# Block-sparse attention with a gated Fourier filter on one core: a reordered opening, work shifted from VectorE to GpSimd and ScalarE, and new places for the first 54 slots

## The chip, the core and the metric

The kernel runs on one core of a Trainium2 chip. A core has a matrix engine (TensorE, PE in the profile, with its weight loads as PEld), three engines for elementwise work (VectorE or DVE, ScalarE or ACT, GpSimd or POOL) and a queue engine (SyncE or SP) that issues most of the DMA transfers. Each engine takes its instructions strictly in the order of its own list and waits for others by semaphores. The metric is the device time of one execution in microseconds.

## The reference, cut to what matters

There are 4 batches of 8 heads with 768 positions and 64 values per head. Each query position takes its own block of 64 keys and the three blocks whose mean key scores best for it, under the causal mask. The output of the attention is then projected three times; the second projection goes through a circular convolution along the sequence, given by a filter in the frequency domain, and the three are multiplied and projected once more.

```python
k_rep = k.reshape(B, H, n_blocks, block, D).mean(axis=3)
gate_scores = np.einsum('bhsd,bhnd->bhsn', q, k_rep)
...
top_idx = np.argsort(gate_scores, axis=-1)[..., -top_k:]
...
scores = scale * np.matmul(q, k.transpose(0, 1, 3, 2))
mask = mask & (pos[:, None] >= pos[None, :])
scores = np.where(mask, scores, -1000000000.0)
...
attn = attn / (np.sum(attn, axis=-1, keepdims=True) + 1e-09)
return np.matmul(attn, v).astype(np.float32)
...
x2_conv = np.fft.irfft(X2 * H, n=S, axis=1)
y = x1 * x2_conv * x3
return (y @ w_out).astype(np.float32)
```

## The kernel before

**Tiles.** Two heads form a pair `p`; there are 16 pairs, four to a batch. Keys, queries and values of a pair are loaded as 128 positions by 6 chunks by 2 heads by 64 (`k_nat`, `q_nat`, `v_nat`, one DMA for each head). Scores are made with the keys' positions on the partitions, so that the exponentials (`ex`) can be used as weights of the product with the values.

**Slots.** The work of one head is cut into three groups of score tiles, of 896 columns each. A group is a slot `n`, and there are 96. In a slot, `scores(n + 1)` is issued on PE, then `exponentials(n)` on ACT with a triangle cut on POOL (line 619), then `products(n - 1)` on PE (line 641). At the end of a head DVE takes a reciprocal and scales the output into `xnat` (lines 649 and 650).

**Order.** The order is written out by hand in the dictionary `ORDER`. A number there is seven times the slot plus one of seven places within it, so a step at 109 is issued in slot 15. A key such as `kc0.3` is a step of pair 3; `kc0:3` is the rule for a pair whose number leaves 3 when divided by four. `open` is the list of what comes before slot 0. `first`, `mid` and `last` place the filter part of batches 0, 1 and 2 among the slots of the next batch; the last batch follows in `tail`. `zeros` gives, for a slot, how many matmuls on zeros of 256 columns are issued ahead of its products (line 635); a `w18` in `open` stands for 18 such matmuls of 128 columns (line 188).

**Preparing a pair.**
- `turn_k` transposes three chunks on PE (line 420); for pairs in `summed` PE also multiplies by `sel`, which gives the block sums (line 422). `cast_k` casts on ACT to `KH` (line 439), `sum_k` reduces or copies on DVE to `krs` (lines 446 and 444). `send_k` moves the halves of `KH` to `KA` and `KB`, by the two engines named in `kcopy` (line 453) or by two DMAs.
- `turn_q`, `copy_q` (ACT, `TQL`, line 501) and `rest_q` (DVE, line 506) do the like for queries; `part_q` copies the second head to `QB`, by the engine in `qcopy` (line 528) or a DMA. From pair 5 on a transposing DMA does the turn, after `cast_q` and `split_q` (lines 513 and 518).
- `prep_kr` makes `bd` and `kr` in three small steps (lines 489 to 493), on DVE for pair 0 and on POOL for the others. `prep_gate` multiplies on PE: 15 matmuls at line 541. `prep_mask` takes the best eight (line 550), compares (`lt`, line 553) and clears the own block (`MN`, line 556), `turn_mask` transposes (line 566). For pairs 0 and 1 the mask goes straight to its rows 64 to 75 of `TQL` and `QB` (lines 569, 575 and 581); for later ones ACT copies it to `M16` (line 577) and two DMAs send it on (`send_mask`).
- `mask_rows` writes the fixed rows of `KA` and `KB` on POOL, the other buffers get them by DMA (`buffer_rows`).

**The Fourier matrices** are built in the opening from sines: products on PE (`sp`, line 223), a rounding on ACT (`sr`, `dft_ka`, line 230), a multiple on POOL (`sm`, `dft_kw`, line 236), the rest on PE (`se`), the sine on ACT (`st`). `twists` takes the sine of three small columns (line 210).

**The filter's spectrum** is prepared during batch 0. `filter_fold` reverses a block of 128 rows on PE (`rev`) and makes sum and difference (`fil`, lines 363 and 364), `spectrum` multiplies and copies (lines 379 and 387), `spectrum_turned` turns (lines 400 to 406). `fold` makes sum and difference of the attention's output for the filter (`xf`, lines 678 and 679). The list `swap` names steps that go to another engine than the usual one.

**Who waits for whom in PSUM.** Transposes, gates, masks and spectra share three banks (`one`), score tiles have two places of two banks, and the output `o` has one bank, so the products of a head wait until the head before has been scaled.

Of the kernel before, what the change touches and what calls it, by code (L numbers as in the profile page):

```python
# [9 lines left out]
FP32 = mybir.dt.float32  # L10
FP16 = mybir.dt.float16
BF16 = mybir.dt.bfloat16
AF = mybir.ActivationFunctionType
ALU = mybir.AluOpType
# [64 lines left out]
    "xact": [], "xpe": [0, 1, 2, 3, 7, 11, 15], "mpool": [], "fpool": [],  # L79
# [30 lines left out]
    "zeros": {23: 9, 17: 2, 10: 5, 19: 8, 2: 3, 18: 3, 6: 3, 26: 2, 7: 4, 15: 1, 8: 5, 37: 1,  # L110
        14: 3, 25: 4, 12: 3, 30: 1, 34: 1, 20: 2, 24: 2, 3: 2, 11: 2},
}


# [1 line left out]
def kernel(  # L116
# [10 lines left out]
    nc = tc.nc  # L127

    B, H, S, D = q.shape
    P = 128  # L130
    SC = S // P
    NB = S // 64
    Dm = H * D
# [23 lines left out]
    hy = ctx.enter_context(tc.tile_pool(name="hy", bufs=1))  # L157
# [127 lines left out]
    id16 = const.tile([P, P], fp, name="id16")  # L285
# [86 lines left out]

    spec = {}

    def spectrum(j, which):
        sl = slice(P * j, P * (j + 1))
        hps = one("hps")
        for i in range(HC):
            nc.tensor.matmul(hps, lhsT=(FC, FS)[which][:, i, sl], rhs=fil[:, which, i, :],
                             start=(i == 0), stop=(i == HC - 1))  # L380
        if which:
            hsb = hy2.tile([P, Dm], FP32, name="hsb", tag="h1")
        else:
            hsb = hy.tile([P, 2, F], FP32, name="hsa", tag="yy",
                          bufs=DC - 1).rearrange("p a f -> p (a f)")[:, 0:Dm]
        spec[j, which] = hsb
        (nc.scalar.copy if (which == 1) != (f"ch{which}{j}" in ORDER["swap"]) else nc.vector.tensor_copy)(
            hsb, hps)

    def spectrum_turned(j, what, part):  # L390
        c, s_ = spec[j, 0], spec[j, 1]
        dst, first, s0, second, s1, op = {
            "A": (Asb[:, j, :], c, tw[:, 0, j:j + 1], s_, tw[:, 1, j:j + 1], ALU.add),
            "B": (Bsb[:, j, :], s_, tw0[:, 0:1] if j == 0 else tw[:, 0, j:j + 1], c,
                  tw[:, 1, j:j + 1], ALU.subtract),
            "2": (A2, c, tw0[:, 0:1], s_, tw0[:, 1:2], ALU.add)}[what]
        if part == 0:
            t = hy.tile([P, Dm], FP32, name="turn", tag="t1", bufs=3)
            if f"ct{what}{j}" in ORDER["swap"]:
                nc.scalar.activation(t, second, AF.Copy, bias=0.0, scale=s1)  # L400
            else:
                nc.gpsimd.tensor_scalar(t, in0=second, scalar1=s1, scalar2=0.0, op0=ALU.mult,
                                        op1=ALU.add)
            spec[j, what] = t
        else:
            nc.vector.scalar_tensor_tensor(out=dst, in0=first, scalar=s0, in1=spec.pop((j, what)),
                                           op0=ALU.mult, op1=op)
# [174 lines left out]
                                scalar2=None, op0=ALU.mult)  # L582

    def send_mask(p):
        nc.sync.dma_start(TQ[p % 3][64:64 + NB, :], M16[p % 2][64:64 + NB, :])
        nc.sync.dma_start(QB[p % 2][64:64 + NB, :], M16[p % 2][96:96 + NB, :])

# [407 lines left out]
```

## Time and profile before

| | |
|---|---|
| median of 3 runs | 243.94 us |
| lowest and highest | 243.31 and 243.98 us |
| the profiled execution's own time | 243.25 us |
| its span | 241.5 us |
| granted clock of TensorE | 1.00 |
| first exponential starts at | 13.89 us |
| 27th exponential (slot 26) starts at | 62.98 us |
| moved by DMA | 38.31 MB, 159 GB/s in the mean |

The span runs from the first to the last recorded instruction; 1.75 us of the execution lie around it. A row of the timeline or of the chain gives a start and a duration; a row of the groups gives, after the bar, the busy time in all and the mean in nanoseconds of one, then the idle time of the engine just before, with what ended it. Instructions that follow each other on one engine overlap a little, so their durations add up to slightly more than the time they take. A matmul of 32-bit values shows as two records. The slot of an exponential is counted from the first, slot 0.

### The profile page before, as it was taken

Reading aid. Unit: us, or ns where it says so; the run is one execution under the profiler, and the core shown is the slowest. Engines: PE = TensorE matmul, PEld = TensorE weight load, DVE = VectorE, ACT = ScalarE, POOL = GpSimd, SP = SyncE. Lnnn points to the kernel's source line nnn. Section 1 sums busy time; section 2 is a strip of 40 time slices with the busy share of each in tenths; the row PEclk is TensorE's granted clock in tenths of the full one; section 3 lists DMA queues with packets and bytes.
Section 4 is the critical chain, followed back from the end, with each engine's and each line's share of the span. In section 5 each row is a group of like instructions: output and inputs, shape, how many; then the busy total and the mean of one; then the engine's idle time right before and its main releaser. Section 6 shows DMA issues by size and latency. Waiting matters only on the chain.

```text
span 241.5 us, 6285 instructions
## 1 busy us (share of the span) xinstructions
PE 228.6 (95%) x2277; PEld 149.5 (62%) x2277; DVE 192.8 (80%) x569; ACT 168.2 (70%) x261; POOL 142.6 (59%) x257
## 2 busy tenths in 40 slices
PE   5789999899899999999999999999999999999993
PEld 4578776577666766666566666666655665544551
DVE  3787797999978999887589978986699767578981
ACT  4879878878878867877985777878854866322341
POOL 8725646588873779853445788736365695006560
PEclk9999999999999999999999999999999999999999
DMA  7999979599999999979989999999961012500015
GB/s 156 218 252 237 176 185 198 113 196 176 185 181 170 189 210 168 173 161 261 246 187 203 144 188 188 154 221 273 175 152 36 10 34 79 186 0 0 3 41 220
DMA packets 108679, 38.31 MB, mean 159 GB/s; under 512 B 100596, under 2 KB 104936, under 8 KB 108648
## 3 DMA queue, kind: packets, MB, share of 16 engines
q1 hardware_dynamic: 106248, 35.68, 75.1%
q0 software_dynamic: 2256, 2.10, 5.9%
q8 instruction: 18, 0.29, 0.5%
q10 hardware_dynamic: 144, 0.13, 0.2%
q14 instruction: 13, 0.11, 0.2%
HBM read 24.64 MB, written 6.29 MB: 128 GB/s over the span
## 4 chain that ended last, share of the span: by engine, by line
PE 81%; DVE 11%; ACT 3%; issue 1%; POOL 1%; ACTq 0%; POOLq 0%; DVEq 0%
PE sps L607 13%; PE x2p L704 9%; PE op L780 8%; PE o L641 7%; PE x3p L768 7%; PE x1p L765 7%; PE xx L717 5%; PE kt L420 3%; PE ye L745 3%; PE yo L748 3%; PE o L635 2%; PE mt L566 2%; PE g L541 2%; DVE m L550 2%; ACT ex L616 2%; PE sps L765 1%
## 5 line engine op out<-in xcount | busy, mean ns | idle before, releaser
L616 ACT ACTIVATE ex<-sps 128x896 f16<-128x896 f32 x96 | 87.6, 923 | 1.6 <-PE sps L607 1.2
L619 POOL TENSOR_SCALAR_AFFINE_SELECT ex<-ex 128x256 f16<-128x256 f16 x96 | 42.3, 444 | 55.7 <-ACT ex L616 48.0
L641 PEld LDWEIGHTS <-ex 128*128 128x128 f16 x672 | 32.2, 97 | 10.4 <-DVE xnat L650 1.5
L641 PE MATMUL o<-V,ex 128*128 128x65 f16 x672 | 35.9, 193 | 0.5 <-DVE xnat L650 0.2
L737 POOL TENSOR_TENSOR yT<-gg,yy 128x384 f16<-128x384 f32 x23 | 22.9, 1016 | 8.1 <-DVE yy L754 3.5
L728 POOL TENSOR_TENSOR PQ<-ta 128x512 f16<-128x512 f32 x12 | 15.2, 1269 | 19.7 <-DVE ta L727 19.6
L607 PE MATMUL sps<-QB,KB 76*128 76x512 f16 (+1 forms) x144 | 26.2, 289 | 0.7 <-ACT ex L616 0.6
L607 PE MATMUL sps<-TQL,KA 76*128 76x512 f16 (+1 forms) x144 | 26.2, 289 | 0.6 <-DVE TQL L569 0.4
L771 ACT CAST x1sb<-x1p 128x384 f16<-128x384 f32 x27 | 12.9, 479 | 16.4 <-PE x1p L765 16.4
L704 PE MATMUL x2p<-wp,xf 128*128 128x512 f16 x96 | 23.8, 378 | 0.0
L765 PE MATMUL x1p<-xT,wp 128*128 128x384 f16 x108 | 22.0, 325 | 0.0
L768 PE MATMUL x3p<-xT,wp 128*128 128x384 f16 x108 | 22.0, 326 | 0.0
L780 PE MATMUL op<-wo,yT 128*128 128x512 f16 x84 | 20.7, 379 | 0.0
L439 ACT CAST KH<-kt 128x384 f16<-128x384 f32 x30 | 14.4, 481 | 8.7 <-DVE krs L446 4.4
L773 DVE TENSOR_TENSOR gg<-x1sb,x3p 128x384 f32<-128x384 f16 x27 | 14.8, 549 | 5.5 <-PE x3p L768 4.7
L650 DVE TENSOR_TENSOR xnat<-o,rc 128x384 f16<-128x384 f32 x32 | 17.8, 557 | 1.1
L768 PEld LDWEIGHTS <-wp 128*128 128x128 f16 x128 | 12.5, 98 | 8.6 <-issue 0.2
L607 PEld LDWEIGHTS <-KA 76*128 76x128 f16 x144 | 12.2, 97 | 8.9 <-issue 1.5
L607 PEld LDWEIGHTS <-KB 76*128 76x128 f16 x144 | 12.4, 98 | 8.3 <-issue 0.7
L420 PE MATMUL kt<-id,k_nat 128*128 128x128 f32 x90 | 16.4, 280 | 0.4 <-DVE TQL L506 0.4
L446 DVE TENSOR_REDUCE krs<-kt 128x6 f32<-128x384 f32 x26 | 14.2, 551 | 2.8 <-PE kt L420 2.3
L550 DVE MAX8 m<-g 128x8 f32<-128x12 f32 x160 | 13.8, 158 | 3.2 <-PE g L541 3.2
(184 smaller groups left out, 490.5 us busy)
## 6 DMA issues: line engine op xcount, KB each, us to landing
q_nat<-in_q_dram SPq DMA_DIRECT2D x32, 192.0 KB
k_nat<-in_k_dram SPq DMA_DIRECT2D x32, 192.0 KB
v_nat<-in_v_dram SPq DMA_DIRECT2D x32, 192.0 KB
out_dram<-osb SPq DMA_DIRECT2D x23, 256.0 KB
wp<-in_moe_w_proj_dram POOLq DMA_DIRECT2D x12, 128.0 KB, 4.2
KA<-KH SPq DMA_DIRECT2D x9, 96.0 KB
KB<-KH SPq DMA_DIRECT2D x9, 96.0 KB
fa<-in_moe_filter_fft_dram SPq DMA_DIRECT2D x3, 256.0 KB
```

The lines of the kernel that those rows point to most:

```text
L420: nc.tensor.transpose(y[:, P * c:P * (c + 1)], chunk, id32)
L550: nc.vector.max(m8[:, c, h, :], g[:, c, h, :])
L607: nc.tensor.matmul(t[:, col:col + q1 - q0], lhsT=kk[0:64 + NB, P * kc:P * (kc + 1)], rhs=qq[0:64 + NB, q0:q1], start=True, stop=True, skip ...
L616: nc.scalar.activation(ex, t[:, 0:W], AF.Exp, bias=0.0, scale=EXPS)
L619: nc.gpsimd.affine_select(out=tri, in_=tri, compare_op=ALU.is_ge, fill=0.0, base=0, pattern=[[0, 2], [1, P]], channel_multiplier=-1)
L641: nc.tensor.matmul(o[:, qc, :], lhsT=ex[:, c0:c0 + P], rhs=V16[p % 3][:, kc, h, 0:65], start=first, stop=False, skip_group_check=True)
L650: nc.vector.tensor_tensor(xn[:, :, D * h:D * (h + 1)], o[:, :, 0:D], rc.to_broadcast([P, SC, D]), op=ALU.mult)
L704: nc.tensor.matmul(pa, lhsT=xf[:, eo, dc, P * i:P * (i + 1)], rhs=wp[:, dc, Dm:2 * Dm], start=(dc == 0), stop=(dc == DC - 1))
L737: e.tensor_mul(st["yT"][:, dc, F * hf:F * (hf + 1)], g, yy[:, 1, ::-1] if hf else yy[:, 0, :])
L765: nc.tensor.matmul(x1p, lhsT=wp[:, d2, dsl], rhs=xT[:, d2, hs], start=(d2 == 0), stop=(d2 == DC - 1))
L768: nc.tensor.matmul(x3p, lhsT=wp[:, d2, 2 * Dm + P * dc:2 * Dm + P * (dc + 1)], rhs=xT[:, d2, hs], start=(d2 == 0), stop=(d2 == DC - 1))
L780: nc.tensor.matmul(op, lhsT=st["yT"][:, cc, P * i:P * (i + 1)], rhs=wo[:, cc, :], start=(cc == 0), stop=(cc == DC - 1))
```

## The change

It changes the order and the engines of steps. What is computed stays the same.

- *Opening.* Keys of pair 0 are loaded, transposed, cast and summed ahead of its queries. The cast of a half comes ahead of its sum in the list. The iotas of the Fourier matrices come ahead of `halves` (three memsets of `sel`). One rounding (`sr1`) comes ahead of `twists`. The warm-up matmuls are 18 + 13 + 7 instead of 21 + 2 + 18 + 6. `flip` leaves the opening for slot 3. Both copies of pair 0's keys are POOL's, ahead of `mask_rows`.
- *Keys and queries.* `kcopy` gives both copies of pairs 0 and 3 to POOL, both of pair 2 to DVE, and of pairs 4, 5 and 6 one to ACT and one to DVE. Pair 5 joins `summed`. The copy of pair 6's second queries moves from DVE to ACT; pair 8 gets ACT for it in place of a DMA and pair 7 a DMA in place of ACT.
- *Masks.* Clearing the own block goes to POOL for pairs 1, 6 and 7 (`mpool`). A new table `mcopy` lets engines do `send_mask` in place of DMAs: ACT and DVE for pair 2, POOL for the second half of pairs 6 and 8.
- *Filter and folds.* For the first of three blocks ACT copies `rev` to SBUF and POOL makes sum and difference (`fl0`). One spectrum copy goes from DVE to ACT (`ch00`), one copy of a turned matrix likewise, one turn goes from POOL to ACT. The difference in `fold` is POOL's for pairs 0 and 7 (`fpool`).
- *Fillers.* The matmuls on zeros ahead of products are 45 instead of 66.
- *Places.* Nearly every step of pairs 1 to 8 and of batch 0's filter part gets a new number, mostly off by one to ten. `mid`, `last` and `tail` stay.

Two new forms come with it: `send_mask` with `mcopy`, and a way of turning straight from PSUM (`scaled`, for a `split` entry in `swap`), which no entry asks for.

```diff
-    "kcopy": {0: 'AV', 1: 'VV', 2: 'PV', 3: 'AV', 4: 'AV', 5: 'VP', 6: 'VP'},
-    "qcopy": {0: 'A', 1: 'V', 2: 'P', 3: 'P', 4: 'P', 5: 'A', 6: 'V', 7: 'A'}, "summed": [2, 6],
-    "xact": [], "xpe": [0, 1, 2, 3, 7, 11, 15], "mpool": [], "fpool": [],
-    "open": ["id32", "halves", "lq0", "lk0", "angles", "twists", "sp0", "lk1", "biasl", "lv0",
-        "period", "sp1", "zeros", "sr0", "flip", "sp2", "own", "lq1", "w21", "sr1", "q0", "sm0",
-        "sr2", "qc0", "biasr", "sm2", "q1", "qc1", "sm1", "MN0", "qr0", "qr1", "k0", "k1", "qd",
-        "ks0", "kc0", "se2", "w2", "ks1", "kr", "kc1", "id16", "se1", "kd", "se0", "lv1", "st2",
-        "st0", "st1", "g", "m", "rows", "w18", "mt", "table", "lk2", "ones", "v", "ma", "lq2",
-        "w6", "mb", "sel16", "s", "late"],
+    "kcopy": {1: 'VV', 2: 'VV', 3: 'PP', 4: 'AV', 6: 'AV', 5: 'AV', 0: 'PP'},
+    "qcopy": {0: 'A', 1: 'V', 2: 'P', 3: 'P', 4: 'P', 5: 'A', 6: 'A', 8: 'A'}, "summed": [2, 5, 6],
+    "xact": [], "xpe": [0, 1, 2, 3, 7, 11, 15], "mpool": [1, 6, 7], "fpool": [0, 7],
+    "mcopy": {8: '-P', 6: '-P', 2: 'AV'},
+    "open": ["id32", "angles", "halves", "lk0", "period", "zeros", "sp0", "lq0", "lv0", "biasl",
+        "sp2", "sp1", "sr1", "twists", "sr2", "w18", "own", "biasr", "lq1", "sm2", "lk1", "sr0",
+        "k0", "sm1", "sm0", "kc0", "MN0", "ks0", "k1", "kc1", "ks1", "id16", "q0", "qc0", "q1",
+        "kr", "qr0", "qc1", "qr1", "kd", "qd", "se1", "se2", "se0", "lv1", "g", "st2", "st1",
+        "st0", "lk2", "rows", "ones", "w13", "m", "table", "v", "mt", "sel16", "ma", "w7", "mb",
+        "late", "lq2", "s"],
...
     "swap": ["mP12", "tB2", "tX13", "tP01", "mC1", "tI2", "tO0", "ctB1", "cIS0", "mC3", "mY02",
...
-        "mC4", "cIC1", "ce03", "ce02", "ce11", "ce00"],
...
+        "cIC0", "fl0", "ctB0", "ch00", "ct20", "cIS2", "ce12", "ce10", "ce00"],
...
-    "zeros": {23: 9, 17: 2, 10: 5, 19: 8, 2: 3, 18: 3, 6: 3, 26: 2, 7: 4, 15: 1, 8: 5, 37: 1,
-        14: 3, 25: 4, 12: 3, 30: 1, 34: 1, 20: 2, 24: 2, 3: 2, 11: 2},
+    "zeros": {23: 1, 10: 2, 19: 4, 2: 1, 6: 3, 7: 6, 8: 5, 14: 2, 25: 6, 12: 3, 24: 4, 36: 2,
+        21: 2, 26: 1, 20: 2, 4: 1},
...
     def send_mask(p):
-        nc.sync.dma_start(TQ[p % 3][64:64 + NB, :], M16[p % 2][64:64 + NB, :])
-        nc.sync.dma_start(QB[p % 2][64:64 + NB, :], M16[p % 2][96:96 + NB, :])
+        for i, dst in enumerate((TQ[p % 3], QB[p % 2])):
+            copy = ENGINES.get(ORDER.get("mcopy", {}).get(p, "--")[i], nc.sync.dma_start)
+            copy(dst[64:64 + NB, :], M16[p % 2][64 + 32 * i:64 + 32 * i + NB, :])
```

The function that the first block's fold goes through, as it stands in both:

```python
        if f"fl{i}" in ORDER["swap"]:

            revs = hy.tile([P, Dm], FP32, name="revs", tag="t1", bufs=3)
            nc.scalar.copy(revs, rev)
            rev, add, sub = revs, nc.gpsimd.tensor_add, nc.gpsimd.tensor_sub
        add(fil[:, 0, i, :], fa[:, i, :], rev)
        sub(fil[:, 1, i, :], fa[:, i, :], rev)
```

More of the change, by code (lines that the diff above doesn't have):

```diff
@@ L373, with scaled @@
     spec = {}
+    def scaled(dst, src, by, act):
+        if act:
+            nc.scalar.activation(dst, src, AF.Copy, bias=0.0, scale=by)
+        else:
+            nc.vector.tensor_scalar(dst, in0=src, scalar1=by, scalar2=None, op0=ALU.mult)
     def spectrum(j, which):
@@ L386, in spectrum @@
         spec[j, which] = hsb
+        if j and f"split{j}" in ORDER["swap"]:
+            state["hps", j, which] = hps
+            scaled(hsb, hps, tw[:, 0, j:j + 1], (which == 1) != (f"ch{which}{j}" in ORDER["swap"]))
+            return
         (nc.scalar.copy if (which == 1) != (f"ch{which}{j}" in ORDER["swap"]) else nc.vector.tensor_copy)(
@@ L390, in spectrum_turned @@
     def spectrum_turned(j, what, part):
-        c, s_ = spec[j, 0], spec[j, 1]
+        c, s_ = spec.get((j, 0)), spec.get((j, 1))
         dst, first, s0, second, s1, op = {
@@ L396, in spectrum_turned @@
             "2": (A2, c, tw0[:, 0:1], s_, tw0[:, 1:2], ALU.add)}[what]
+        if j and f"split{j}" in ORDER["swap"]:
+            if part == 0:
+                spec[j, what] = t = hy.tile([P, Dm], FP32, name="turn", tag="t1", bufs=3)
+                scaled(t, state.pop(("hps", j, what == "A")), s1, f"ct{what}{j}" in ORDER["swap"])
+            else:
+                e = nc.vector if f"cg{what}{j}" in ORDER["swap"] else nc.gpsimd
+                e.tensor_tensor(dst, first, spec.pop((j, what)), op=op)
+            return
         if part == 0:
```

84 rows, old and new, of the table ORDER are left out of this document.

## The prediction

> **What bounds the kernel now.** I read the page's busy shares first, then the busy time in six stages cut at points where the chain of waits changes character, then that chain, and last the timeline of the opening.
>
> ```profile
> PE 228.6 (95%) x2277; PEld 149.5 (62%) x2277; DVE 192.8 (80%) x569; ACT 168.2 (70%) x261; POOL 142.6 (59%) x257
> ```
>
> ```profile
> 0.00:13.89 13.89, 9.09 (x92) 7.22 (x93) 7.68 (x48) 8.64 (x16) 9.47 (x33) 1.00 1.13 191
> 13.89:29.10 15.21, 14.09 (x193) 11.76 (x192) 12.68 (x58) 13.46 (x22) 8.60 (x21) 1.00 1.12 237
> 29.10:41.97 12.87, 12.65 (x145) 9.02 (x143) 10.12 (x34) 10.23 (x16) 6.62 (x15) 1.00 0.85 180
> 41.97:50.00 8.03, 6.81 (x82) 4.53 (x80) 7.86 (x26) 6.49 (x9) 4.40 (x10) 1.00 0.67 129
> 50.00:62.98 12.98, 12.86 (x163) 10.30 (x164) 12.21 (x35) 10.52 (x15) 11.72 (x21) 1.00 1.01 188
> 62.98:122.00 59.02, 58.20 (x608) 37.66 (x606) 48.74 (x145) 47.32 (x72) 37.57 (x66) 1.00 1.10 192
> ```
>
> The columns are the stage, its length, then PE, PEld, DVE, ACT, POOL, the granted clock and DMA. After 63 us PE is full (58.20 of 59.02), so whatever is won or lost before that shifts the rest unchanged. Up to 13.89 us no engine is full: that stage is a chain. From 13.89 to 62.98 PE idles 1.12 + 0.22 + 1.22 + 0.12 = 2.7 us in all, and in 41.97 to 50.00 VectorE is the full one (7.86 of 8.03). But "PE busy" here includes matmuls on zeros, and they stand on the chain itself:
>
> ```profile
> 3.83 2.35 PE warm L188 x21
> 7.37 0.94 DVE TQL L506 x2
> 8.31 0.94 DVE krs L446 x2
> 41.97 0.69 DVE fil L363
> 52.11 0.88 PE o L635 x8
> 54.12 0.32 DVE KA L453
> 57.54 0.12 PE kt L422 x2
> 58.84 0.98 PE o L635 x9
> ```
>
> A filler of line 635 costs PE 0.88 / 8 = 0.11 us, a warm-up matmul of line 188 2.35 / 21 = 0.112, and a matmul of line 422 that sums a chunk of keys 0.12 for its two records.
>
> **The opening, up to the first exponential.** These rows set its pace.
>
> ```profile
> 0.82 1.28 ACT L210 ACT_TABLE_LOAD   x1 [0.82 <-PEq L981]
> 1.33 0.10 POOL L256 MEMSET sel<- 128x2 f32 x1
> 1.79 0.44 POOL L199 IOTA vals<- 1x384 f16 x1
> 2.69 1.14 PE L223 MATMUL sps<-vals 1*128 1x384 f16 x3 [2.69 <-POOL vals L201]
> 2.85 0.21 ACT L210 ACTIVATE tw<-twf 128x6 f32<-128x6 f32 x1 [0.75 <-POOL twf L208]
> 3.54 1.25 ACT L230 ACTIVATE dft_ka<-sps 128x384 f32<-128x384 f32 x3 [0.49 <-PE sps L223]
> 5.97 1.16 PE L420 MATMUL qt<-id,q_nat 128*128 128x128 f32 x6
> 6.84 0.87 ACT L501 ACTIVATE TQL<-qt 128x384 f16<-128x384 f32 x2 [2.05 <-PE qt L420]
> 8.80 0.94 ACT L439 CAST KH<-kt 128x384 f16<-128x384 f32 x2 [0.22 <-DVE krs L446]
> 9.27 0.32 DVE L489 TENSOR_TENSOR bd<-krs,sel 128x24 f32<-128x24 f32 x1
> 9.84 0.18 DVE L493 TENSOR_TENSOR kr<-bd,kr 128x24 f16<-128x24 f32 x1
> 9.86 0.72 PE L541 MATMUL g<-kr,TQL 128*128 128x24 f16 x15 [0.81 <-DVE kr L492]
> 13.89 0.92 ACT L616 ACTIVATE ex<-sps 128x896 f16<-128x896 f32 x1 [0.84 <-PE sps L607]
> ```
>
> PE. The iotas now come ahead of the three memsets of sel, so PE can begin 1.79 - 1.33 = 0.46 earlier, and three warm matmuls fewer save 0.34: the first transposes could start at 5.97 - 0.80 = 5.17. Keys take the first place in SP's queue, which the queries had; the chain ran through the warm-up, not through that load, so the queries were there by 5.97, how much sooner the rows don't say. Between 5.17 and 5.97 I take the early end.
>
> ACT. A first dft_ka now stands ahead of the twists' sine, and the compiled program has a third table load: one at the start, a second between the first dft_ka and tw. The first dft_ka takes the third product instead of the first, two thirds of 1.14 later: 3.54 - 0.46 + 0.76 = 3.84. Then 1.25 for the three, 1.28 for the load and 0.21 for tw: ACT is free for the key casts at 6.58. Transposes at 5.17 would ask for them 6.84 - 5.97 = 0.87 later, at 6.04, so the load gives back 0.54. The casts begin 0.26 ahead of the old 6.84. Bounds of the extra load: 0 if the transposes keep 5.97 or later, 1.28 if they are early and nothing else covers it.
>
> [...]
>
> DVE. The work is the same: two reductions 0.94, three kr steps from 9.27 to 10.02 = 0.75, two query rests 0.94, in all 2.63, now in the order reductions, kr, rests. It starts at 7.37 - 0.26 = 7.11 and would end at 9.74. Of the 15 gate matmuls 9 come after the last rest, 0.72 x 9 / 15 = 0.43, so the gate would be done at 10.17 against 9.86 + 0.72 = 10.58. Alone this makes the first exponential 0.41 earlier, at 13.48. That casts go ahead of sums is worth no more than the 0.22 that ACT waited for krs.
>
> POOL. The two key copies of pair 0 were on ACT and DVE, off the chain; both are POOL's now. These rows, of the timeline, of line 556 and of the groups, decide what that does.
>
> ```profile
> 26.93 0.82 POOL L483 CAST V<-v_nat 128x768 f16<-128x768 f32 x1
> 27.00 0.83 DVE L556 TENSOR_TENSOR MN<-lt,ownm 128x120 f16<-128x120 f16 x1
> L556 DVE TENSOR_TENSOR MN<-lt,ownm x16: 221/223/931, 11.8 to 183.3; 128x120 f16<-128x120 f16 x16
> L453 POOL COPY KB<-KH 64x768 f16<-64x768 f16 x2 | 1.6, 824 | 0.1
> L236 POOL TENSOR_SCALAR dft_kw<-dft_ka 128x384 f16<-128x384 f32 x3 | 1.5, 511 | 0.0
> 5.81 0.29 POOL L826 CAST id<-id 128x128 f16<-128x128 f32 x1
> ```
>
> MN takes 0.223 in the median but 0.83 where it starts 0.07 after a POOL cast, and ends as that cast ends: held by 0.61. POOL has its second dft_ka at 3.84 + 0.42 + 1.28 + 0.21 + 0.42 = 6.17, then three dft_kw of 0.51 and the cast of id16, 0.29: the copies run from about 8.0 to 8.8 and 8.8 to 9.6. DVE reaches its first kr step at 7.11 + 0.94 = 8.05, just behind the first copy. Two holds of 0.61 make +1.22. The bounds are no hold (if DVE is first and POOL waits) and four (all three kr steps and MN, which falls beside the mask rows that POOL now makes after the copies): 0 to 2.44. I take two, since the third step meets a memset. First exponential: 13.48 + 1.22 = 14.7, that is +0.8; bounds -0.4 and +2.0.
>
> [...]
>
> **The slots.** The diff's "zeros" go from 66 to 45: 21 x 0.11 = -2.31. Of these 20 lie ahead of 63 us, where the chain ran through the two longest, x8 (now 4) and x9 (now 1). Summing pair 5 on PE adds six pairs of records: 6 x 0.12 = +0.72. Four rows of the groups, one of the timeline and one of the chain price the rest.
>
> ```profile
> L387 DVE COPY hsa<-hps 128x512 f32<-128x512 f32 x3 | 2.0, 681 | 0.0
> L728 POOL TENSOR_TENSOR PQ<-ta 128x512 f16<-128x512 f32 x12 | 15.2, 1269 | 19.7 <-DVE ta L727 19.6
> L575 ACT ACTIVATE TQL<-mt 12x768 f16<-12x768 f16 x1 | 0.8, 801 | 0.1
> L453 ACT COPY KA<-KH 64x768 f16<-64x768 f16 x3 | 2.5, 827 | 0.1
> 32.14 0.41 POOL L619 TENSOR_SCALAR_AFFINE_SELECT ex<-ex 128x256 f16<-128x256 f16 x1
> 34.80 0.21 PE o L641 x7
> ```
>
> On DVE only what stood in its full stretches counts: one spectrum copy goes to ACT (-0.68, in 41.97 to 50.00), and the KA copy at 54.12 leaves it (-0.32). The filter's first block (two operations of 0.69) leaves DVE in 29.10 to 41.97, where DVE had 2.75 us free: worth nothing. On POOL those two cost 1.27 each, by line 728, and need a copy of rev on ACT first; behind them wait the triangle cuts of line 619, whose products PE takes up later: the cut that ended at 32.55 was wanted at 34.80, a cover of 2.2 us (without it, +2.5). Folds and masks on POOL are off both chains, at nothing, under the same cover. Pair 3's two key copies also go to POOL, 2 x 0.82 beside DVE's chain of about 30 to 32 us: one hold, +0.6 (0 to 1.2). ACT gains pair 2's mask rows, 0.80, and an IS copy, but loses pair 3's KA copy, 0.83; its 10.23 of 12.87 leave room, with a serial loss of 0.3 (0 to 0.8). Four small mask DMAs fewer on SP and the changed load order move nothing: PE, DVE and POOL waited hardly for loads. Past 63 us one filler, -0.1, is in the 2.31.
>
> Sum of the slots: -2.31 + 0.72 - 0.68 - 0.32 + 0.6 + 0.3 = -1.7. With the opening, +0.8 - 1.7 = -0.9. The profiled execution took 243.25 (span 241.5), so the changed one should take **242.3**. The median of the three runs shown is 243.94, 0.7 above; 0.3% of it, 0.73, is about what a measurement tells from no change, so faster means below 243.2, slower above 244.7.
>
> **Rivals.**
>
> 1. *The whole gain.* DVE's kr steps go ahead of POOL's copies and nothing is held: the opening -0.4, the slots without pair 3's hold (0.6) and ACT's loss (0.3) -2.6, so 243.25 - 3.0 = 240.3. For it: DVE and POOL are only 0.05 apart by my count. Against: the MN row.
> 2. *GpSimd as the holder.* Every hold decides: opening +2.0, pair 3 +1.2, sums +0.72, and fillers give back only the 11 of the stretch after 50 us, -1.2: 243.25 + 2.7 = 246.0. It decides from the point where DVE's first kr step starts after POOL's first key copy. [...]
> 3. *Fillers only filled waits.* PE then waits where it used to multiply zeros; the opening's +0.8 meets DVE's -1.0: 243.1, no change. For it: the fillers lie exactly in the stretches where DVE is near full. Against: products follow x8 and x9 on the chain with no wait.
>
> **How the numbers follow.** Forecast 0.44 (its own range 241.4 to 243.3), whole gain 0.17, no change 0.18, GpSimd 0.21. Faster: 0.40 of the forecast and 0.17, 0.57. Same: 0.04 and 0.16, 0.20. Slower: 0.21 and 0.02, 0.23. The range 239.9 to 245.5 leaves out about 0.05 below and 0.13 above.
>
> **What would show it.** A table load of 1.28 between two dft_ka; key transposes near 5.2; bd and the kr cast stretched to 0.6 to 0.9 beside POOL's KA and KB copies; the first exponential near 14.7; 45 fillers, and slot 26's exponential about a microsecond earlier than 62.98; PE full after that and a like tail. The forecast is wrong if the first exponential is before 13.6 or after 15.5, if g, products or scores wait for POOL by more than a microsecond in all, or if PE idles more than 2.7 us from the first exponential to slot 26.

## The result, and the profile after

| | before | after |
|---|---|---|
| median | 243.53 us (20 runs) | 245.02 us (20 runs) |
| lowest and highest | 243.16 and 245.06 | 244.17 and 248.17 |
| the profiled execution's own time | 243.25 us | 245.31 us |
| its span | 241.5 us | 243.6 us |
| its granted clock of TensorE, mean | 1.00 | 0.983 |
| its first exponential | 13.89 us | 15.30 us |

The ratio is 1.0057, 95% interval 1.0039 to 1.0075: the changed kernel is slower, by 0.0057 x 244 = 1.4 us, where 0.9 us of gain was forecast. Runs more than 1.5% above the fastest of their kernel (248.17 here, one in run d below) are left out of the ratios and of the mean clocks. The two profiled executions lie 2.06 us apart, more than the medians do: the one of before took 0.28 less than its median, the one of after 0.29 more. Shifts read from the two traces overstate the loss by some 0.6.

The busy shares, first the page's summary of after:

```profile
PE 230.2 (95%) x2259; PEld 150.4 (62%) x2259; DVE 189.8 (78%) x559; ACT 172.6 (71%) x268; POOL 147.7 (61%) x266
```

PE holds fewer instructions than before (2259 against 2277), yet was busy 1.6 us longer (230.2 against 228.6). The work on VectorE shrank by 3.0 us, as the change meant it to. Why fewer matmuls take longer is seen in the windows of one microsecond in the opening of after. The columns are PE, PEld, DVE, ACT, POOL with the instructions in brackets, then the granted clock, the DMA share and GB/s:

```profile
8.00:9.00 1.00, 0.42 (x4) 0.20 (x2) 0.96 (x2) 0.97 (x3) 0.94 (x2) 1.00 1.20 225
9.00:10.00 1.00, 0.46 (x6) 0.21 (x6) 0.97 (x4) 1.00 (x4) 0.94 (x2) 1.00 1.21 215
10.00:11.00 1.00, 0.85 (x18) 0.75 (x17) 0.54 (x5) 0.98 (x3) 0.86 (x3) 0.64 1.10 203
...
16.00:17.00 1.00, 1.00 (x6) 0.66 (x5) 0.53 (x4) 0.59 (x2) 0.41 (x1) 0.50 1.02 258
17.00:18.00 1.00, 1.00 (x15) 0.84 (x14) 0.97 (x4) 0.83 (x2) 0.00 (x0) 0.95 0.86 306
```

PE is busy less than half of 8 to 10 us; then TensorE's clock falls to 0.50 and stays there until 17.1 us. Every stage of before has 1.00 there. The timeline of the same stretch, in start, duration, engine and line (the lines of after lie 1 to 21 further down than those of before):

```profile
3.92 1.28 ACT L211 ACT_TABLE_LOAD   x1
5.21 0.21 ACT L211 ACTIVATE tw<-twf 128x6 f32<-128x6 f32 x1
5.28 1.51 PE L440 MATMUL kt<-id,k_nat 128*128 128x128 f32 x6
6.19 0.48 ACT L459 CAST KH<-kt 128x384 f16<-128x384 f32 x1
7.54 0.81 POOL L473 COPY KA<-KH 64x768 f16<-64x768 f16 x1
8.01 0.39 DVE L509 TENSOR_TENSOR bd<-krs,sel 128x24 f32<-128x24 f32 x1
8.42 0.82 POOL L473 COPY KB<-KH 64x768 f16<-64x768 f16 x1
8.43 0.84 DVE L512 CAST kr<-bd 128x24 f16<-128x24 f32 x1
9.33 0.39 PE L561 MATMUL g<-kr,TQL 128*128 128x24 f16 x2 [0.91 <-ACT QB L548]
11.88 0.82 POOL L304 COPY KB<-KA 12x768 f16<-12x768 f16 x1
11.97 0.80 DVE L576 TENSOR_TENSOR MN<-lt,ownm 128x120 f16<-128x120 f16 x1
14.36 0.91 PE L628 MATMUL sps<-TQL,KA 76*128 76x512 f16 x3
15.30 0.92 ACT L637 ACTIVATE ex<-sps 128x896 f16<-128x896 f32 x1 [3.54 <-PE sps L628]
```

Three things stand there. The keys' transposes begin at 5.28, as worked out (5.17). VectorE's small steps are held beside GpSimd's copies: bd 0.39, the kr cast 0.84 (0.18 before) and MN 0.80 (0.22 before), each ending 0.03 to 0.07 after the copy beside it. MN's is the copy of the mask rows, which the copies of the keys have pushed back to 11.88 (10.27 in run c below). The gate's matmuls wait 0.91 meanwhile. It is put down to QB, but kr, which they need, was late as well: in run e below, with the same opening, a wait of 1.02 at this place is put down to the kr cast. And the three score matmuls that took 0.54 before take 0.91, at half clock.

What became of these delays is read from the first scaling of a head's output into `xnat`, which comes once in three slots. The starts in the profiled executions, and those of four experiments below:

| slot | before | after | a | d | e | g |
|---|---|---|---|---|---|---|
| 2 | 20.55 | 21.78 | 20.30 | 21.08 | 21.62 | 20.37 |
| 32 | 76.45 | 75.97 | 74.44 | 75.26 | 75.80 | 74.57 |
| 53 | 120.76 | 122.14 | 119.48 | 120.89 | 120.84 | 120.36 |
| 95 | 205.90 | 207.18 | 204.51 | 205.92 | 205.87 | 205.12 |

After starts 1.23 late, is 0.48 ahead by slot 32, and 1.38 late again at slot 53; from there on it runs as before. A single one of these shifts is uncertain, since the steps stand in another order: in slot 26 after's scaling comes 1.59 later than before's, its exponential about 1.5 earlier. In the lost stretch PE waits where it did not before, by its timeline of after:

```profile
78.64 0.81 PE L738 MATMUL xx<-x2eo,FC 128*128 128x512 f16 x3 [0.54 <-ACT x1sb L792]
93.69 0.54 PE L628 MATMUL sps<-TQL,KA 76*128 76x512 f16 x3 [0.36 <-DMA TQL<-M]
```

Two suspects follow: the opening with its clock, and transfers that the new places put later.

### The profile page after: what moved, and what is told of

It is laid out like the page before. It is cut to its first block, busy times and chain, and to the rows that moved or that the text cites. A ratio compares the mean times of both kernels' runs of the same rounds, so it can differ in the third digit from the quotient of the medians.

```text
span 243.6 us, 6253 instructions
## 1 busy us (share of the span) xinstructions
PE 230.2 (95%) x2259; PEld 150.4 (62%) x2259; DVE 189.8 (78%) x559; ACT 172.6 (71%) x268; POOL 147.7 (61%) x266
## 4 chain that ended last, share of the span: by engine, by line
PE 72%; ACT 8%; DVE 6%; DMA 5%; POOL 4%; issue 3%; SPq 0%; POOLq 0%; DVEq 0%; ACTq 0%
PE sps L628 11%; PE op L801 8%; PE x2p L725 7%; PE o L662 6%; PE x1p L786 6%; PE x3p L789 6%; PE xx L738 4%; PE kt L440 4%; ACT ex L637 4%; DMA TQL<-q 3%; PE ye L766 2%; PE yo L769 2%; PE g L561 2%; PE mt L586 2%; PE warm L189 1%
## 5 line engine op out<-in xcount | busy, mean ns | idle before, releaser
L628 PE MATMUL sps<-TQL,KA 76*128 76x512 f16 (+1 forms) x144 | 26.7, 296 | 0.8 <-DMA TQL<-M 0.4
L628 PEld LDWEIGHTS <-KA 76*128 76x128 f16 x144 | 12.7, 100 | 10.4 <-issue 2.3
L440 PE MATMUL kt<-id,k_nat 128*128 128x128 f32 x90 | 18.3, 302 | 0.0
L628 PEld LDWEIGHTS <-KB 76*128 76x128 f16 x144 | 12.4, 98 | 8.2
L466 DVE TENSOR_REDUCE krs<-kt 128x6 f32<-128x384 f32 x24 | 13.2, 551 | 4.9 <-ACT KH L459 2.6
```

The costliest lines, as they stand in the source:

```text
L440: nc.tensor.transpose(y[:, P * c:P * (c + 1)], chunk, id32)
L628: nc.tensor.matmul(t[:, col:col + q1 - q0], lhsT=kk[0:64 + NB, P * kc:P * (kc + 1)], rhs=qq[0:64 + NB, q0:q1], start=True, stop=True, skip ...
```

## The experiments

Each was timed in five rounds beside the kernel before. A ratio's interval is about 0.002 wide to each side, so two ratios can be told apart from some 0.003, or 0.7 us. In the listings of these kernels the line numbers are 24 or 25 lower than in after.

**The change in two halves.** Run a keeps the changed slots and takes the opening of before; run b does the reverse.

```diff
 a, against after
-    "kcopy": {..., 0: 'PP'}
+    "kcopy": {..., 0: 'AV'}
-    "open": [list of after]
+    "open": [list of before]
 b, against before
-    "kcopy": {0: 'AV', ...}
+    "kcopy": {0: 'PP', ...}
-    "open": [list of before]
+    "open": [list of after]
```

> The changed kernel with the opening of before (its list, and pair 0's keys copied by ACT and DVE); slots and engines stay changed. If the opening alone makes the change slower: first exponential at 13.9, the clock 1.00 all through, and about 1.4 us less than the changed kernel, so near the kernel before, ratio 1.000. If the new slots cost something of their own: still above 1.003. If they gain and the opening hid it: below 0.997.

> The kernel before with the changed opening alone (its list, pair 0's keys copied by POOL). If the opening's 1.4 us reaches the end, 1.006. If the slots have waits in which a late start is made up for, 1.000 to 1.003. The first exponential is at 15.3 in either case.

Run a came to 0.9943 (0.9922 to 0.9965), 242.70 us; b to 1.0040 (1.0024 to 1.0056). Run b lies between the two values that had been expected for it. So the slots alone gain 1.4 us and the opening loses. But the two do not add up: ahead of the changed slots the opening costs 1.0057 - 0.9943 = 0.0114, that is 2.8 us; ahead of the old ones 1.0 us. Runs m and n return to this.

**The clock.** Run d puts twelve warm matmuls into the gap ahead of the gate's matmuls and changes nothing else.

```diff
-        ... "se0", "lv1", "g", ...
+        ... "se0", "lv1", "w12", "g", ...
```

> The changed kernel with twelve more warm-up matmuls on zeros ahead of the gate, where PE waits for kr anyway; the holds stay. If PE's idling between 8 and 10 us makes the clock fall: it stays at 1.00, and the first exponential comes 0.6 to 0.9 us earlier, at 14.4 to 14.7, ratio about 1.003. If the clock has another cause: no change, 1.006.

It came to 0.9982 (0.9967 to 0.9997), 1.8 us better than after and more than expected. Three windows and the timeline of d:

```profile
8.00:9.00 1.00, 1.00 (x9) 0.60 (x8) 0.96 (x2) 0.80 (x2) 0.94 (x2) 1.00 1.39 218
9.00:10.00 1.00, 0.83 (x18) 0.69 (x16) 0.97 (x4) 1.00 (x3) 0.94 (x2) 1.00 1.38 218
10.00:11.00 1.00, 0.85 (x22) 0.75 (x21) 0.57 (x5) 0.98 (x3) 0.86 (x3) 1.00 1.39 217
```

```profile
8.44 0.84 DVE L488 CAST kr<-bd 128x24 f16<-128x24 f32 x1
8.76 0.83 PE L165 MATMUL warm<-zeros 128*128 128x128 f16 x12
...
11.95 0.82 DVE L552 TENSOR_TENSOR MN<-lt,ownm 128x120 f16<-128x120 f16 x1
...
14.67 0.92 ACT L613 ACTIVATE ex<-sps 128x896 f16<-128x896 f32 x1 [2.71 <-PE sps L604]
```

The holds are still there in full, but the clock in this execution was 1.00 throughout the opening, and the first exponential came at 14.67, 0.63 before that of after. That this is the clock and no other effect of the matmuls is borne out by run m below: it has the opening of after without them, its clock happened to fall only at 14.44, and its first exponential came at 14.73. The matmuls make falls rarer and do not rule them out. Half clock for the shorter time measured below (3.4 us in a span of 242) lowers an execution's mean clock to about 0.993; 17 of 19 executions of after are at 0.993 or below, and 6 of 11 of d. In the profiled execution of run n, which has the opening of d, the clock fell at 14.88. Even so, work that computes nothing, put where PE waited, was worth about as much as taking the holds away, as the next run shows.

**The keys' copies.** Run c gives pair 0's copies back to ScalarE and VectorE and leaves the order of the opening as changed.

```diff
-    "kcopy": {..., 0: 'PP'}
+    "kcopy": {..., 0: 'AV'}
```

> The changed kernel, pair 0's two key copies back on ACT and DVE, all else as changed. If the holds by POOL set the opening: the cast of kr 0.18 instead of 0.84, MN 0.22 instead of 0.80, first exponential 1.2 to 1.8 us earlier, at 13.5 to 14.1, ratio 1.000. If the lowered clock sets it and does not come from the holds: first exponential at 14.5 or later and the clock still 0.50 from 10 to 17 us.

It came to 0.9998 (0.9980 to 1.0016), 1.4 us better than after. The timeline of c:

```profile
8.14 0.28 DVE L488 CAST kr<-bd 128x24 f16<-128x24 f32 x1
...
11.55 0.22 DVE L552 TENSOR_TENSOR MN<-lt,ownm 128x120 f16<-128x120 f16 x1
14.21 0.92 ACT L613 ACTIVATE ex<-sps 128x896 f16<-128x896 f32 x1 [1.47 <-PE sps L604]
```

With GpSimd's copies of the keys gone MN takes 0.22 again and the kr cast 0.28: the copies made the holds. The 14.21 lies 0.1 outside the range expected, and the clock fell in this execution too, from 11.96 to 15.38. What c and d gain is not cleanly holds and clock, though. Without the holds PE waits less (of 8 to 10 us it is busy 1.84 in c, 0.88 in after), and the clock is higher over the timed executions: its mean was 0.987 in after, and 0.995 in c as in d.

**Both mended.** Run g has the copies as in c and the warm matmuls as in d, moves the step that issues the keys' halves (`kd`) behind `mt`, and has the late places of run e.

```diff
-    "kcopy": {..., 0: 'PP'}
+    "kcopy": {..., 0: 'AV'}
-        ... "qr1", "kd", "qd", "se1", "se2", "se0", "lv1", "g", ... "mt", ...
+        ... "qr1", "qd", "se1", "se2", "se0", "lv1", "w12", "g", ... "mt", "kd", ...
```

> The changed kernel with its early key work kept, but three things mended: the first KA and KB copies by ScalarE and VectorE in place of GpSimd, twelve warm matmuls ahead of g, and the keys' cast issue after the trees; the late places as before. If the holds by GpSimd's copies and the clock are all that the opening loses: kr cast 0.2, MN 0.2, clock 1.00 throughout, first exponential at 13.0 to 13.9, ratio 0.990 to 0.994. If the order itself (keys first) is what loses: first exponential at 14.2 or later though the clock stays 1.00, ratio 0.996 to 1.000.

It came to 0.9921 (0.9902 to 0.9940), 242.06 us: 3.3 us better than after, about what c and d gain together (1.4 + 1.8). Its mean clock over the timed executions was 0.999. The timeline of g:

```profile
8.14 0.29 DVE L488 CAST kr<-bd 128x24 f16<-128x24 f32 x1
...
8.88 0.98 PE L165 MATMUL warm<-zeros 128*128 128x128 f16 x12
...
11.54 0.22 DVE L552 TENSOR_TENSOR MN<-lt,ownm 128x120 f16<-128x120 f16 x1
11.79 0.86 DVE L449 COPY KB<-KH 64x768 f16<-64x768 f16 x1
...
13.87 0.92 ACT L613 ACTIVATE ex<-sps 128x896 f16<-128x896 f32 x1 [1.08 <-PE sps L604]
```

The first exponential comes 0.80 ahead of d's. That is not yet the holds' price at full clock: in this execution VectorE's copy to KB took 0.86 and stood ahead of the mask's write into TQL, and the queries' transposes ended at 8.13. Runs k and l below have the same opening and reached the first exponential at 13.14 and 13.24, l with a copy of 0.36 and transposes that ended at 7.87:

```profile
13.24 0.92 ACT L613 ACTIVATE ex<-sps 128x896 f16<-128x896 f32 x1 [0.72 <-PE sps L604]
```

So the holds cost between 0.8 and 1.5 us of the opening at full clock, by three executions. With g the intended gain is there, and more than the 0.9 us forecast: 1.9 us against the kernel before. It does not stand apart from a and f, whose intervals overlap its own, so what the keys-first order itself is worth in time is not settled; by the ratios it can be 0.4 us.

**Transfers that come later.** Runs e and f put the issue of pair 7's keys, three transfers of wp and the turn of pair 7 back to their old places, e in the changed kernel, f in run a.

```diff
-    'kd.7': 259, 'wp02': 206, 'wp03': 205, 'wp23': 192, 'tc.7': 191, 'tr.7': 191
+    'kd.7': 256, 'wp02': 184, 'wp03': 185, 'wp23': 182, 'tc.7': 194, 'tr.7': 194
```

> The changed kernel with the places of pair 7's key issue, of wp's transfers on SP's queue and of the transpose at 191 as they were before (256, 184, 185, 182, 194). Opening as changed, so its 15.30 to the first exponential and 2.1 us of cost stay. Theory one (the loss in slots 33 to 53 comes from what was moved on SP's queue): TensorE's waits on a transposing DMA at 93.69 and on x1sb at 78.64 go, the shift against the kernel before is +1.28 at slot 53 less 0.5 to 1.0, ratio 1.001 to 1.003. Theory two (the loss in slots 33 to 53 comes from the half clock and the late start of the opening alone, since the run with the twelve warm matmuls ahead of g ended it): the waits stay or move, shift at slot 53 stays within 0.2 of +1.28, ratio 1.005 to 1.007.

> The kernel of a_open_before (list of the opening and the first key copy as before, slots as changed) with the late places as before too (256, 184, 185, 182, 194). Theory one: of the -2.01 at slot 32 less is given back than the 0.6 that a_open_before lost on to slot 95 (it ended at -1.39), ratio 0.991 to 0.994. Theory two: the late places are worth nothing where the opening is undisturbed, ratio 0.994 to 0.996, shift to the end -1.2 to -1.4.

Run e came to 1.0051 (1.0026 to 1.0076), f to 0.9937 (0.9920 to 0.9954): neither differs from its partner (1.0057, 0.9943). In e's profiled execution the two waits of 0.54 and 0.36 were gone and slot 53 came 1.3 earlier than in after, as theory one had it, but the times do not follow; g, which has the same late places, shows a wait of 0.57 on x1sb at 77.28. One execution's trace had suggested a cause that five rounds do not bear out. A few tenths remain possible. Run e shows something else, in its windows:

```profile
12.00:13.00 1.00, 0.17 (x3) 0.18 (x4) 0.77 (x1) 0.00 (x0) 0.93 (x5) 1.00 1.39 218
13.00:14.00 1.00, 1.00 (x12) 0.86 (x9) 0.50 (x1) 0.00 (x0) 0.94 (x4) 0.52 1.38 218
...
16.00:17.00 1.00, 1.00 (x8) 0.65 (x7) 0.56 (x1) 0.43 (x2) 0.41 (x1) 0.78 1.10 291
```

The opening's instructions are the same as in after, yet the clock fell at 13.04 rather than 10.28, and for half as long.

**The fillers and the moved work.** Run h gives the kernel before the 45 fillers of the change and nothing else; run i gives run a the 66 of before.

```diff
 h, against before
-    "zeros": {23: 9, 17: 2, 10: 5, ...}
+    "zeros": {23: 1, 10: 2, 19: 4, ...}
 i, against a: the reverse
```

> The kernel before with the changed list of fillers alone (45 in place of 66). If the 21 fillers lay on TensorE's path, each is worth its duration and the kernel ends 1.5 to 2.3 us earlier, ratio 0.991 to 0.994, at a granted clock of 1.00. If they sat in waits of TensorE, ratio 0.999 to 1.001. If they kept the clock up, it falls below 1.00 in the opening or the first slots and the ratio is above 1.001.

> The kernel of a_open_before (slots as changed, list of the opening and the first key copy as before, ratio 0.9943), but with the 66 fillers of the kernel before. It completes a square: the 45 fillers alone came to 1.0009, the changed slots with 45 to 0.9943. If TensorE's fillers lie on its path once VectorE is relieved, the 21 extra ones cost 1.5 to 2.3 us here and the ratio is 1.000 to 1.004. If they sit in waits here too, the ratio stays at 0.993 to 0.996, and the whole 1.39 us of the slots comes from moved work.

| | 66 fillers | 45 fillers |
|---|---|---|
| slots as before | 1 | 1.0009 (0.9993 to 1.0025) |
| slots as changed | 1.0007 (0.9997 to 1.0017) | 0.9943 (0.9922 to 0.9965) |

Neither half of the slots' change is worth anything alone; the two together give 1.4 us. The other half is all that the slots change besides the fillers, moved work and new places alike. The windows from 18 to 24 and from 24 to 63 us suggest why, first of before, then of h, i and a:

```profile
18.00:24.00 6.00, 5.78 (x88) 4.84 (x87) 4.78 (x24) 5.65 (x10) 3.43 (x7) 1.00 1.02 238
24.00:63.00 39.00, 36.96 (x456) 27.68 (x453) 34.57 (x111) 31.47 (x47) 26.70 (x55) 1.00 0.91 177
```

```profile
18.00:24.00 6.00, 5.43 (x79) 4.33 (x78) 4.88 (x23) 5.65 (x10) 3.47 (x9) 1.00 0.96 233
24.00:63.00 39.00, 36.01 (x445) 26.57 (x445) 34.57 (x113) 32.26 (x49) 26.68 (x55) 1.00 0.88 172
```

```profile
24.00:63.00 39.00, 36.89 (x465) 28.16 (x464) 31.09 (x106) 34.36 (x53) 28.00 (x57) 1.00 0.91 170
```

```profile
24.00:63.00 39.00, 36.79 (x461) 27.68 (x460) 31.85 (x108) 35.19 (x53) 28.62 (x57) 1.00 0.98 176
```

In h, PE's busy time falls by 0.35 + 0.95 = 1.3 us and its idle time grows by as much: without the fillers PE waits where it multiplied zeros. By the profile's waits from 18 to 63 us these are 2.3 us for VectorE, 0.4 for ScalarE and 0.3 for GpSimd, where before has 1.6, all for VectorE, whose 34.57 of 39 us stay as they are. In i, VectorE is relieved by 3.5 us and PE is as busy as ever, partly with zeros. In a, PE is as busy as in i with fewer zeros, so it holds more useful work, and slot 32 comes 2.01 earlier than before. How much of the second half is VectorE's relief and how much the new places was not tried apart; run l below takes some of the relief back and loses nothing.

**Three small terms of the forecast**, each against run g (0.9921).

```diff
 j: sine of the twists first
-        "sp2", "sp1", "sr1", "twists", "sr2", ...
+        "sp2", "sp1", "twists", "sr1", "sr2", ...
 k: pair 3's keys off GpSimd
-    "kcopy": {..., 3: 'PP', ...}
+    "kcopy": {..., 3: 'AV', ...}
 l: GpSimd relieved
-    "mpool": [1, 6, 7], "fpool": [0, 7], "swap": [..., "fl0", ...]
+    "mpool": [], "fpool": [], "swap": [...]
```

> The kernel of g_mended_opening (0.9921) with the twists' sine ahead of the first rounding step, so that the table load between two dft_ka goes. The forecast's term was that this load gives back 0.54 us: ratio 0.9899, first exponential 0.5 earlier. If the keys' transposes and not ScalarE set the start of the casts (6.10), ratio 0.991 to 0.993 and the first exponential within 0.2 of that kernel's 13.87.

> The kernel of g_mended_opening (0.9921) with pair 3's two key copies by ScalarE and VectorE, as before the change. The forecast charged one hold of 0.61 us by GpSimd's copies: ratio 0.9896. If those copies fall beside nothing that sets the end, 0.991 to 0.993; if ScalarE and VectorE can't take them without loss there, 0.994 or more.

> The kernel of g_mended_opening (0.9921) with the filter's first block of sums, the masks of pairs 1, 6 and 7 and the folds 0 and 7 back on VectorE. The forecast costed all of these moves at nothing: ratio 0.991 to 0.993. If VectorE's relief is what the slots gained (two sums of 0.69, three masks of 0.22, two folds), the ratio rises to 0.994 to 0.998. If GpSimd's share held VectorE up, the ratio falls to 0.990 or less.

Run j came to 0.9932 (0.9917 to 0.9946), l to 0.9918 (0.9898 to 0.9938): no difference from g. In l VectorE was busy for 32.77 of the 39 us from 24 to 63, in g for 32.01. Run k came to 0.9950 (0.9932 to 0.9967), 0.7 us slower than g, which is just more than the two intervals leave open (0.6), and not to be told from j. In j, without the load between two dft_ka, the first exponential and the first cast of the keys stand where they stood, by its timeline:

```profile
6.10 0.48 ACT L435 CAST KH<-kt 128x384 f16<-128x384 f32 x1 [0.80 <-PE kt L416]
...
13.86 0.92 ACT L613 ACTIVATE ex<-sps 128x896 f16<-128x896 f32 x1 [1.15 <-PE sps L604]
```

ScalarE simply waits 0.80 for the keys' transposes; the casts began at 6.09 or 6.10 in g, k and l as well, with the load in its place. (The first exponential alone would not show it, since it came at 13.14 in k.) And k's timeline shows what GpSimd's two copies of pair 3 may spare:

```profile
28.78 0.83 ACT L449 COPY KA<-KH 64x768 f16<-64x768 f16 x1
...
30.17 0.55 PE L416 MATMUL qt<-id,q_nat 128*128 128x128 f32 x3 [0.59 <-DVE krs L442]
31.83 0.54 PE L604 MATMUL sps<-TQL,KA 76*128 76x512 f16 x3 [0.16 <-ACT ex L613]
```

The copy of 0.83 is back among ScalarE's exponentials, and PE waits there, 0.59 for VectorE's sum of the keys and 0.16 for an exponential; g has neither wait.

**What the opening costs, and where.** Run m is the changed kernel with 66 fillers; run n is run b with the twelve warm matmuls of d.

```diff
 m, against after
-    "zeros": {23: 1, 10: 2, 19: 4, ...}
+    "zeros": {23: 9, 17: 2, 10: 5, ...}
 n, against b
-        ... "se0", "lv1", "g", ...
+        ... "se0", "lv1", "w12", "g", ...
```

> The changed kernel with the 66 fillers of the kernel before. It is to i_slots_all_fillers (1.0007) what the changed kernel (1.0057) is to a_open_before (0.9943), where the opening cost 2.8 us. If the opening's cost is the same whatever the slots, ratio 1.010 to 1.014. If slots with all fillers have slack that takes part of it up, as those of the kernel before seem to have (b_open_after lost only 0.98 us), ratio 1.003 to 1.007, and 21 fillers are worth nothing behind the changed opening.

> The kernel of b_open_after (1.0040) with twelve warm matmuls ahead of g, which in the changed kernel were worth 0.0075 of the ratio. If the half clock in the opening costs as much before the old slots, ratio 0.995 to 0.998. If the old slots take up most of what the clock loses, ratio 1.001 to 1.004.

Run m came to 1.0066 (1.0045 to 1.0087), n to 1.0021 (1.0004 to 1.0038). So the opening costs 1.0066 - 1.0007 = 0.0059, 1.4 us, ahead of the changed slots with all fillers, between the 2.8 with 45 fillers and the 1.0 ahead of the old slots; the warm matmuls that were worth 1.8 us in the changed kernel are worth 0.5 in b, which the intervals can't tell from nothing. The likely reading is that a late start counts in full where PE has little else in its way, and less where fillers and VectorE hold PE up anyway. That the fillers take part is shown (a difference of 1.3, uncertain by 0.9); by which waits the old slots take the delay up is not, since b's trace shows a shift that stays at 2.1 from slot 2 to slot 53.

Runs f, h and i also show how far one trace can be trusted. They have the opening of before, instruction for instruction up to the first exponential, and reach it at 14.31, 14.44 and 14.43 us; before and a reach it at 13.89. The opening of g spreads as far: 13.87, 13.14 and 13.24 in g, k and l.

## Why the prediction was wrong

The forecast was -0.9 us: +0.8 for the opening and -1.7 for the slots. Measured by the halves it is +2.8 and -1.4. The sign went with the opening.

*The step that failed: the opening's sum has no term for TensorE's clock.* "Two holds of 0.61 make +1.22 ... First exponential: 13.48 + 1.22 = 14.7" treats a hold as plain delay, and "three warm matmuls fewer save 0.34" counts warm matmuls as cost alone. The holds left PE with 0.42 and 0.46 us of work in two microseconds, the clock went to half for 6.8 us, and the first exponential came at 15.30. With the gap filled, in run d, it came at 14.67, where the forecast had it; at 14.68 in n, and at 14.73 in m, where the clock fell late. That edit is worth 1.8 us of time (uncertain by 0.6), the largest part of the 2.0 by which the opening was mis-sized. No rival had the clock either. The second rival named the right holder and the right start, the first kr step behind the first copy, but for 246.0 it priced holds only.

*The signs.* None of the three signs by which the forecast was to be known wrong showed in after's trace. The first exponential at 15.30 lies between 13.6 and 15.5, PE waited 0.2 us for GpSimd at g, and it idled 2.2 us from the first exponential to slot 26, not 2.7. Slot 26's exponential even came earlier, at about 61.5 against 62.98. The signs watch for idle time, and at half clock PE counts as busy: 1.00 of the microsecond from 16 to 17 us, at a clock of 0.50. That what is won or lost before 63 us shifts the rest unchanged is not borne out either: by the same traces the kernel ended 2.1 us later.

*The holds.* That VectorE's small steps are held beside GpSimd's copies was right, and the price nearly so: bd 0.21, the kr cast 0.66 and MN 0.58 over their usual 0.18, 0.18 and 0.22 make 1.45, three holds, where two of 0.61 were taken. MN had been put among the bounds. The third kr step, for which no hold was taken, had none: at 9.31, beside GpSimd's memset (9.30 to 10.03), it took 0.18, as before the change.

*The start.* Transposes at 5.28 against 5.17 and casts at 6.19 against 6.58. The extra table load was charged 0.54; run j shows about nothing, since the keys' transposes set the casts. In after the load ends at 5.20, and tw starts 0.01 later, at 5.21. A load charged 0.54 that costs nothing and a third hold that was not charged go against each other, so that 14.7 was met at full clock is in part luck.

*The slots.* The sum was near (-1.7 against -1.4), its terms were not. "21 x 0.11 = -2.31" for the fillers is +0.2 alone (h), and the moved work, costed at +0.6, is +0.2 with all fillers (i). The two are one term, not two: a filler stands on the path only once the rest has moved. Ahead of the changed slots the 21 fillers are worth 1.6 us (i against a) where 2.31 was taken, and that the sum came near is in part luck, since the moved work was priced too dear by 0.4. The third rival was right about the slots as they were, and wrong about them as changed. Pair 3's copies on GpSimd were charged 0.6 for a hold; they look worth 0.7 the other way (k, at the edge of the intervals); that ScalarE and VectorE were the tighter ones there is argued from two waits of one trace. The sums, masks and folds on GpSimd cost and gain nothing, as forecast (l). That the load order moves nothing could not be refuted (e, f). Pair 5's sums on PE, the spectrum copy moved to ScalarE and ScalarE's own loss were not tried alone.

## What to carry to other kernels

Where a reordering makes TensorE wait for a microsecond or two, read the granted clock of the next ten microseconds before adding up durations: here the half clock behind the waits cost as much as the waits, and twelve matmuls that compute nothing, put into the gap, won back as much as taking the holds away (1.8 us in run d, 1.4 in run c). Price edits together that act on the same waits: the thinner fillers and the rest of the slots' change were worth nothing each and 1.4 us together. And do not explain a loss by the waits of one trace until a timed run without those waits is faster.

## What the runs showed of the hardware

In the openings of these traces the half clock lasted for 3.4 us or for twice that. From the windows, with the share of each edge's microsecond taken from its granted clock, it lasted from 10.28 to 17.10 (6.82) in after and from 13.04 to 16.44 (3.40) in e; in the other runs whose clock fell in the opening it was 6.82 in b and 3.42 in each of c, m and n. With the same opening it fell at 10.28, 13.04 and 14.44 in after, e and m, and how much a kernel loses changes from execution to execution: the 20 runs of after spread from 244.17 to 248.17, and the two slowest (247.52 and 248.17) had the lowest mean clock, 0.972. PE was not idle ahead of the falls: in the 3.4 us before each of the six it was busy between 48% and 64% by the profile. In d it was busy for 48% of the stretch from 10.85 to 14.25, in before for 61% of that from 9.0 to 12.4, and both kept their clock, so no threshold can be read from these runs.
